# x tiles by chunk pairs, second value weights in quarters and one more warm-up matmul in the opening of a state-space and memory-attention kernel

## Chip, cores and metric

The kernel runs on one core of a Trainium2 chip. The metric is the device time of one execution in microseconds. All runs below are in the same (fast) state. The changed kernel was measured beside runs of the kernel before on the same chip.

## The reference, cut to what matters

Two independent parts, joined along the last axis. Part A is a diagonal complex state-space layer over 2048 steps. Part B is attention in segments of 32 rows with 8 memory rows, 32 heads of width 128:

```python
v = jnp.einsum('btd,dhe->bhte', h, Wv)     # h: 8 memory rows and 32 rows of x
...
o = jnp.einsum('bhqk,bhke->bhqe', p, v)
o = jnp.einsum('bhte,hed->btd', o, Wo)     # its first 8 rows are the next memory
```

The change touches only how the kernel begins, with the products of x and the value weights `Wv` for the first 512 rows of x and the first two groups of four heads.

## The kernel before

The value matmuls take x with its 1024 features on the partitions, in eight chunks of 128. For the first 512 rows the kernel loads x by rows and transposes on TensorE; later rows arrive through transposing loads. `wvs[0]` and `wvs[1]` are the value weights of the first two head groups, eight chunks of 128 KB each. Two queues issue, SyncE (`k.SP`) and ScalarE (`nc.scalar`).

```python
for t in range(4):                       # a tile of 128 rows, and two chunks of weights
    for j in range(2):
        b.load_rows(t, xr, q2[j], slice(j * 512, j * 512 + 512))
    for j in range(2):
        b.load_wv(0, wvs[0], KC, q2[j], [2 * t + j])
for j in range(2):                       # second weights, two halves of 512 KB
    b.load_wv(1, wvs[1], 2, q2[j], [j])
...                                      # parameters, memory, transposing loads of x from row 512 on
for i in range(7):                       # warm-up on constants
    k.PE.matmul(pw[:, i % 2, :], one[:, 0:128], one, start=True, stop=True)

def v_first(self, w, xr, e):             # the first four row tiles
    p = [k.ps("A") for t in range(4)]
    for t, todo in enumerate((((0, 0, 2),), ((0, 2, 4), (1, 0, 4)), ((0, 4, 6), (1, 4, 6), (2, 0, 6)),
                              ((0, 6, 8), (1, 6, 8), (2, 6, 8), (3, 0, 8)))):
        self.turn_rows(t, xr)            # 8 transposes, 2 evictions
        for tt, c0, c1 in todo:          # (tile, chunks c0 to c1)
            self.v_mm(p[tt], tt, w, range(c0, c1))
    ...
```

After `v_first` come three groups of eight matmuls on the second weights, then a 24-row matmul that turns the parameters of part A. This "parameter matmul" is the mark used below: all work in front of it belongs to the opening. That work is 56 matmuls of 512 columns (32 in `v_first`, 24 in the groups) and 32 transposes.

Of the kernel before, what the change touches and what calls it, by code (L numbers as in the profile page):

```python
# [8 lines left out]
FP32 = mybir.dt.float32  # L9
BF16 = mybir.dt.bfloat16  # L10
# [14 lines left out]
PC = 8; TB = 512; NB = 4  # L25
# [108 lines left out]
class PartA:  # L134
# [11 lines left out]
    def params(self, pool, tmp):  # L146
        k = self.k; V, S, PE, nc = k.V, k.S, k.PE, k.nc
        r24 = tmp[0:3 * PC, 1536:1664]
        pr = k.ps("O")[:, 0, :]
        PE.matmul(pr[:, 0:3 * PC], r24, k.ident[0:3 * PC, 0:3 * PC], start=True, stop=True)  # L150
        raw = pool.tile([128, 3, PC], FP32, name="a_raw", bufs=1)
        V.tensor_copy(raw[:].rearrange("p a c -> p (a c)"), pr[:, 0:3 * PC])
        lre = raw[:, 0, :]; lim = raw[:, 1, :]

        def small(name):
            return pool.tile([128, PC], FP32, name=name, bufs=1)
        dtb = pool.tile([128, PC], BF16, name="a_dtb", bufs=1)
        S.activation(dtb[:], raw[:, 2, :], ACT.Exp)
        dt = small("a_dt"); V.tensor_copy(dt[:], dtb[:])
        are = small("a_are"); V.tensor_tensor(are[:], dt[:], lre, ALU.mult)  # L160
        tht = small("a_tht"); V.tensor_tensor(tht[:], dt[:], lim, ALU.mult)
        rr = small("a_rr"); S.activation(rr[:], are[:], ACT.Exp)
        turn = small("a_turn"); V.tensor_scalar(turn[:], tht[:], 1.0 / (2.0 * math.pi), None, ALU.mult)
        fr = small("a_fr8"); V.tensor_scalar(fr[:], turn[:], MAGIC, None, ALU.add)
        V.tensor_scalar(fr[:], fr[:], MAGIC, None, ALU.subtract)
        V.tensor_tensor(fr[:], turn[:], fr[:], ALU.subtract)
        s1 = small("a_s1"); S.activation(s1[:], fr[:], ACT.Sin, scale=TWO_PI_LO)
        V.scalar_tensor_tensor(fr[:], fr[:], -1.0, fr[:], ALU.mult, ALU.max)
        c1 = small("a_c1"); S.activation(c1[:], fr[:], ACT.Sin, scale=-TWO_PI_LO, bias=k.hpb[:])
        nre = small("a_nre"); V.tensor_tensor(nre[:], rr[:], c1[:], ALU.mult)  # L170
        V.tensor_scalar(nre[:], nre[:], 1.0, None, ALU.subtract)
        nim = small("a_nim"); V.tensor_tensor(nim[:], rr[:], s1[:], ALU.mult)
        den = small("a_den"); V.tensor_tensor(den[:], lre, lre, ALU.mult)
        t0 = small("a_t0"); V.tensor_tensor(t0[:], lim, lim, ALU.mult)
        V.tensor_tensor(den[:], den[:], t0[:], ALU.add)
        V.reciprocal(den[:], den[:])
        V.tensor_scalar(den[:], den[:], 2.0, None, ALU.mult)
        bre = small("a_bre"); V.tensor_tensor(bre[:], nre[:], lre, ALU.mult)
        V.tensor_tensor(t0[:], nim[:], lim, ALU.mult)
        V.tensor_tensor(bre[:], bre[:], t0[:], ALU.add)  # L180
        V.tensor_tensor(bre[:], bre[:], den[:], ALU.mult)
        bim = small("a_bim"); V.tensor_tensor(bim[:], nim[:], lre, ALU.mult)
        V.tensor_tensor(t0[:], nre[:], lim, ALU.mult)
        V.tensor_tensor(bim[:], bim[:], t0[:], ALU.subtract)
        V.tensor_tensor(bim[:], bim[:], den[:], ALU.mult)
        nbre = small("a_nbre"); V.tensor_scalar(nbre[:], bre[:], -1.0, None, ALU.mult)
        self.rr, self.turn, self.bre, self.nbre, self.bim = rr, turn, bre, nbre, bim
        ji = pool.tile([128, TB + 1], I32, name="a_k1", bufs=1)
        k.G.iota(ji[:], pattern=[[1, TB + 1]], base=0, channel_multiplier=0)
        V.tensor_copy(self.jf, ji[:])  # L190
# [126 lines left out]
class PartB:  # L317
# [21 lines left out]
    def init(self, tmp, pm):  # L339
        k = self.k  # L340
        k.V.memset(self.accE[:], 0.0)
        m0 = tmp[0:M, 0:D]
        for c in range(KC):
            k.PE.matmul(pm[:, c * M:(c + 1) * M], tmp[0:M, c * 128:(c + 1) * 128], k.ident[0:M, 0:M], start=True, stop=True)
        self.memT = self.xe[:, :, T:XE]
        k.V.memset(self.memT, 0.0)
        k.V.tensor_copy(self.m0T[:], pm[:, 0:KC * M].rearrange("p (c m) -> p c m", c=KC))
        k.V.tensor_copy(self.memT[:, :, 0:NMX + 1], self.m0T[:])
# [19 lines left out]
            if lo < hi:  # L368
                k.SP.dma_start(self.xe[:, :, lo:hi], self.x[0][lo + r:hi + r, :], transpose=True)

    def load_rows(self, t, xr, e, cs=slice(0, D)):
        self.k.tc.keep_in_program_order(e.dma_start(xr[:, t, cs], self.x[0][t * 128 + 64:t * 128 + 192, cs]))

    def turn_rows(self, t, xr):

        k = self.k
        pt = k.ps("O", (128, 2, 1024), BF16)
        for c in range(KC):
            k.tc.keep_in_program_order(k.PE.transpose(pt[:, c // 4, (c % 4) * 128:(c % 4) * 128 + 128], xr[:, t, c * 128:(c + 1) * 128], k.ident[:]))
        for i in range(2):  # L380
            k.copy("v", self.xe[:, 4 * i:4 * i + 4, t * 128:(t + 1) * 128], pt[:, i, 0:512].rearrange("p (c n) -> p c n", c=4))

    def sum_x(self, q, pool):

# [47 lines left out]
    def v_pair(self, hb, q, w, e):  # L432
# [8 lines left out]
        self.v_st(hb, q, st, e)  # L441
        yield

    def v_first(self, w, xr, e):

        k = self.k
        p = [k.ps("A") for t in range(4)]
        for t, todo in enumerate((((0, 0, 2),), ((0, 2, 4), (1, 0, 4)), ((0, 4, 6), (1, 4, 6), (2, 0, 6)),
                                  ((0, 6, 8), (1, 6, 8), (2, 6, 8), (3, 0, 8)))):
            self.turn_rows(t, xr)  # L450
            for tt, c0, c1 in todo:
                self.v_mm(p[tt], tt, w, range(c0, c1))
        for q in range(2):
            st = self.v_tile()
            for i in range(2):
                k.copy("s", st[:, i, :], p[2 * q + i][:])
                if i == 0:
                    yield
            self.v_st(0, q, st, e)
            yield  # L460
# [409 lines left out]
def kernel_main(tc, A_x, A_Lre, A_Lim, A_Bre, A_Bim, A_Cre, A_Cim, A_logdt, A_Dskip, B_x, B_mem0, B_Wq, B_Wk, B_Wv, B_Wo, out,  # L870
                force=False, dbg=None):
    with ExitStack() as ctx:
        k = K(tc, ctx)
        k.dbg = dbg
        nc = k.nc
        consts(k)
        a = PartA(k, A_x, A_Lre, A_Lim, A_Bre, A_Bim, A_Cre, A_Cim, A_logdt, A_Dskip, out)
        b = PartB(k, B_x, B_mem0, B_Wq, B_Wk, B_Wv, B_Wo, out)
# [10 lines left out]
        with pool("p1", "right") as p1:  # L889
            tmp = a.hsp.tile([128, 2 * PC * TB], BF16, name="a_hs", bufs=4)  # L890
            w01 = a.hsp.tile([128, 2 * PC * TB], BF16, name="a_hs", bufs=4)
            wvs = {i: w01[:, 4096 * i:4096 * i + 4096].rearrange("p (a b) -> p a b", a=KC) for i in range(2)}
# [4 lines left out]
            a.jf = b.rall[:, 0:TB + 1]  # L897
            xr = tmp[:, 4096:8192].rearrange("p (t d) -> p t d", t=4)
            q2 = (k.SP, nc.scalar)
            for t in range(4):  # L900
                for j in range(2):
                    b.load_rows(t, xr, q2[j], slice(j * 512, j * 512 + 512))
                for j in range(2):
                    b.load_wv(0, wvs[0], KC, q2[j], [2 * t + j])
            for j in range(2):
                b.load_wv(1, wvs[1], 2, q2[j], [j])
            a.load_params(tmp)
            k.SP.dma_start(tmp[0:M, 0:D], b.mem0[0])
            b.load_x(512, 1024)
            b.load_x(1024, 1536)  # L910
            b.load_x(1536, T)
            one = nc.const_aps.tensor(1.0, [128, 512], BF16)
            pw = k.ps("O")
            for i in range(7):
                k.PE.matmul(pw[:, i % 2, :], one[:, 0:128], one, start=True, stop=True)

            def values():
                yield from b.v_first(wvs[0], xr, k.SP)
                for hb, q in [(1, 0), (1, 1)] + [(hb, q) for q in range(2, 8) for hb in range(2)]:
                    yield from b.v_pair(hb, q, wvs[hb], k.SP)  # L920
                for hb in range(2, HB):
                    for q in range(8):
                        if q == 1 and hb + 1 < HB and hb + 1 not in wvs:
                            wvs[hb + 1] = b.load_wv(hb + 1)
                        yield from b.v_pair(hb, q, wvs[hb], k.SP)
            v = values()
# [76 lines left out]
        with pool("p3", "right") as p3:  # L1003
            b.p3 = p3
            b.qk_init(p3)
            pr, at = b.proj(), b.attention()
# [8 lines left out]
            for n, (hp, u) in enumerate(at):  # L1015
# [4 lines left out]
                if u == 4 and 8 <= hp < 12:  # L1020
                    w = k.w8((8, 512), "wo0")
# [117 lines left out]
```

## Time and profile before

| | before |
|---|---|
| median time (first three runs) | 1241.64 us |
| span of the traced run | 1240.4 us |
| TensorE busy | 1230.1 us |
| parameter matmul starts | 20.77 us |

The profile page of the kernel before: the busy times of the engines (first line) and the shares of the chain of work that ended last (second line).

```profile
PE 1230.1 (99%) x8078; PEld 654.6 (53%) x8148; DVE 610.7 (49%) x1124; ACT 326.0 (26%) x754; POOL 211.6 (17%) x290
...
PE 98%; DMA 1%; issue 0%; DVE 0%
```

TensorE is the limit, and only 1% of the chain is a transfer. The list of TensorE waits of the kernel before, over the whole span (microseconds in total, times, longest):

```profile
PE psO L379 <- DMA a_hs<-in_B_x_dram: 0.9, 1, 0.9
PE psO L915 <- PEq L1120: 0.8, 1, 0.8
PE psS L414 <- DMA a_hs<-in_B_Wv_dram: 0.6, 1, 0.6
PE psS L414 <- DVE b_xe L77: 0.5, 1, 0.5
```

All four lie in the first 16 us. The TensorE timeline of the opening before: start, duration, operation, count, and in brackets the idle time. L915 is the warm-up, L379 a transpose, L414 a value matmul, L150 the parameter matmul.

```profile
0.85 3.07 PE L915 MATMUL psO<-const-bfloat16-1.0 128*128 128x512 bf16 x7 [0.85 <-PEq L1120]
3.76 0.62 PE L379 MATMUL psO<-ident,a_hs 128*128 128x128 bf16 x8
4.90 0.61 PE L414 MATMUL psS<-a_hs,b_xe 128*128 128x512 bf16 x2 [0.52 <-DVE b_xe L77]
6.42 0.62 PE L379 MATMUL psO<-ident,a_hs 128*128 128x128 bf16 x8 [0.92 <-DMA a_hs<-in_B_x_dram]
...
13.00 1.89 PE L414 MATMUL psP<-a_hs,b_xe 128*128 128x512 bf16 x8
15.49 1.90 PE L414 MATMUL psS<-a_hs,b_xe 128*128 128x512 bf16 x8 [0.60 <-DMA a_hs<-in_B_Wv_dram]
...
20.77 0.18 PE L150 MATMUL psO<-ident,a_hs 24*128 24x24 bf16 x1
```

Read the starts rather than the durations. At full clock a 512-wide matmul starts every 216 ns (each is recorded as 0.38 us long, so neighbours overlap), a transpose every 56 ns, as between 7.62 and 8.92 us in this trace. So after the two matmuls at 4.90 TensorE could have gone on at 5.33, and it went on at 6.42, when the second row tile had landed. One number sums up an opening:

**excess = (start of the parameter matmul - start of the first transpose) - 13.9 us**, where 13.9 = 56 x 0.216 + 32 x 0.056 is the work in between.

Before it is 20.77 - 3.76 - 13.9 = 3.1 us.

### The profile page before, as it was taken

What the parts mean: (1) busy time and instruction counts of PE and PEld (TensorE: products, weight loads), DVE (VectorE), ACT (ScalarE), POOL (GpSimd) and SP (SyncE); (2) the same over time, 40 slices, a digit from 0 to 9 for tenths busy, and PEclk for the clock granted to TensorE, in tenths of its full rate; (3) what the DMA queues carried; (4) which work ended last, traced back from release to release, by engine and by line L of the source; (5) the groups of instructions that cost most, each with busy time, mean ns of one, the idle gap of its engine ahead of it and who ended that gap; (6) DMA issues with size and microseconds to landing.
All of it is one profiled execution on the core that took longest, in us unless ns stands there. A gap on an engine that the chain in (4) does not pass through costs nothing.

```text
span 1240.4 us, 19648 instructions
## 1 busy us (share of the span) xinstructions
PE 1230.1 (99%) x8078; PEld 654.6 (53%) x8148; DVE 610.7 (49%) x1124; ACT 326.0 (26%) x754; POOL 211.6 (17%) x290
## 2 busy tenths in 40 slices
PE   8999999999999999999999999999999999999998
PEld 4444444444455445566666655655565554454444
DVE  4889999999941122444444444444444550011000
ACT  3344334444310001332333333333333230000000
POOL 2000000000032144222222222232222330000000
PEclk9999999999999999999999999999999999999999
DMA  9942232333666558577668554645575469707000
GB/s 220 261 132 66 87 94 68 102 94 77 153 187 203 154 166 164 106 151 149 134 128 170 124 136 96 128 77 104 106 139 106 73 203 218 153 18 153 17 18 28
DMA packets 306056, 153.95 MB, mean 124 GB/s; under 512 B 147242, under 2 KB 299810, under 8 KB 305962
## 3 DMA queue, kind: packets, MB, share of 16 engines
q1 hardware_dynamic: 304138, 150.82, 52.6%
q10 hardware_dynamic: 1824, 1.84, 0.5%
q8 instruction: 65, 1.06, 0.4%
q14 instruction: 29, 0.24, 0.1%
HBM read 73.70 MB, written 44.71 MB: 95 GB/s over the span
## 4 chain that ended last, share of the span: by engine, by line
PE 98%; DMA 1%; issue 0%; DVE 0%
PE psP L587 33%; PE psS L687 9%; PE psO L256 9%; PE psS L414 9%; PE psP L414 9%; PE psP L687 5%; PE psP L310 4%; PE psS L310 4%; PE psP L570 4%; PE psO L631 3%; PE psS L613 3%; PE psO L687 2%; PE psS L720 1%; PE psP L505 1%; PE psP L739 1%; DMA a_hs<-in_B_Wv_dram 1%
## 5 line engine op out<-in xcount | busy, mean ns | idle before, releaser
L587 PE MATMUL psP<-b_xe,w 128*128 128x480 bf16 x2048 | 439.3, 366 | 0.0
L587 PEld LDWEIGHTS <-w 128*128 128x128 bf16 x2048 | 193.9, 98 | 183.0
L620 POOL TENSOR_TENSOR b_m<-b_e,maskB 99x396 bf16<-99x396 bf16 x160 | 139.4, 871 | 347.5 <-ACT b_e L616 347.5
L77 DVE CAST b_q<-psP 128x480 bf16<-128x480 f32 (+1 forms) x192 | 98.0, 531 | 145.3 <-PE psP L587 133.8
L414 PEld LDWEIGHTS <-b_xe 128*128 128x128 bf16 x1024 | 99.8, 98 | 121.7 <-DMA a_hs<-in_B_Wv_dram 1.1
L75 ACT ACTIVATE b_k<-psP 128x480 bf16<-128x480 f32 x128 | 73.1, 571 | 318.7 <-PE psP L587 318.7
L687 PEld LDWEIGHTS <-b_ol 128*128 128x128 bf16 x960 | 93.1, 98 | 109.3
L616 ACT ACTIVATE b_e<-psS 99x396 bf16<-99x396 f32 x176 | 87.4, 497 | 170.5 <-PE psS L613 161.7
L638 DVE TENSOR_TENSOR b_ot<-psO,b_rall 99x512 bf16<-99x512 f32 x176 | 121.6, 691 | 6.4
L256 PE MATMUL psO<-w,a_bt 128*128 128x512 bf16 x496 | 114.7, 379 | 0.8
L636 DVE RECIPROCAL b_rall<-psO 99x4 f32<-99x4 f32 x176 | 31.1, 177 | 132.5 <-PE psO L631 132.5
L687 PE MATMUL psS<-w,b_ol 128*128 128x512 bf16 x406 | 91.5, 379 | 0.6
L414 PE MATMUL psS<-w,b_xe 128*128 128x512 bf16 x378 | 90.1, 379 | 0.4
L414 PE MATMUL psP<-w,b_xe 128*128 128x512 bf16 x376 | 89.8, 379 | 0.4
L256 PEld LDWEIGHTS <-a_bt 128*128 128x128 bf16 x512 | 49.7, 98 | 59.0
L310 PEld LDWEIGHTS <-a_hs 128*128 128x128 bf16 x512 | 49.5, 98 | 58.3
L77 DVE CAST b_ost<-psS 128x512 bf16<-128x512 f32 x13 | 9.0, 691 | 125.4 <-PE psS L687 125.4
L631 PE MATMUL psO<-b_v,b_m 128*128 128x129 bf16 x704 | 70.0, 221 | 0.0
L613 PEld LDWEIGHTS <-b_k 128*128 128x128 bf16 x704 | 50.0, 98 | 33.9 <-DVE b_k L77 0.2
L613 PE MATMUL psS<-b_q,b_k 128*128 128x99 bf16 x704 | 60.1, 208 | 0.1
L75 ACT ACTIVATE b_vst<-psS 128x512 bf16<-128x512 f32 x56 | 33.4, 597 | 99.1 <-PE psS L414 70.2
L353 POOL MEMSET b_z<- 32x128 bf16 x1 | 0.2, 194 | 341.3 <-DVE a_hs L292 341.3
(205 smaller groups left out, 1162.3 us busy)
## 6 DMA issues: line engine op xcount, KB each, us to landing
b_v<-b_vx SPq DMA_DIRECT2D x16, 1056.0 KB
b_os<-b_ot SPq DMA_DIRECT2D x16, 960.0 KB
w<-in_B_Wv_dram SPq DMA_DIRECT2D x14, 1024.0 KB
b_vx<-b_vst SPq DMA_DIRECT2D x48, 256.0 KB
w<-in_B_Wo_dram SPq DMA_DIRECT2D x12, 1024.0 KB
w<-in_B_Wq_dram SPq DMA_DIRECT2D x16, 512.0 KB
w<-in_B_Wk_dram SPq DMA_DIRECT2D x16, 512.0 KB
a_xn<-in_A_x_dram SPq DMA_DIRECT2D x32, 128.0 KB
```

The costliest lines, as they stand in the source:

```text
L75: self.S.activation(out, in_, ACT.Copy)
L77: self.V.tensor_copy(out, in_)
L256: m = PE.matmul(u[:, i, :], self.bt[:, i, c, :], self.xT[tb][:, c, :], start=(c == 0), stop=(c == KC - 1))
L310: PE.matmul(py[:], self.hs[tb][:, pc, i, tt * 128:(tt + 1) * 128], self.ct[half, i][:, pc, :], start=(pc == 0 and i == 0), stop=(pc == PC ...
L414: m = self.k.PE.matmul(p[:], self.xe[:, c, t * 128:(t + 1) * 128], w[:, c, :], start=(c == 0), stop=(c == KC - 1))
L587: PE.matmul(p[:, 0:480], w[:, i * KC + c, hh * 128:(hh + 1) * 128], self.xe[:, c, 480 * q:480 * q + 480], start=(c == 0), stop=(c == KC - 1))
L613: PE.matmul(s[:, j * GW:(j + 1) * GW], kt[:, hh, g0:g0 + 128], qt[:, hh, g0:g0 + GW], start=True, stop=True)
L616: k.S.activation(e[:], s[0:GW, 0:4 * GW], ACT.Exp, scale=float(E) ** -0.5, accum_out=self.accE[0:GW, i:i + 1])
L620: k.G.tensor_tensor(v4(m[0:GW, 0:4 * GW]), v4(e[:]), mask[0:GW, :, :].unsqueeze(2).to_broadcast([GW, 2, 2, GW]), ALU.mult)
L631: PE.matmul(o[:, gg, cs], m[:, j * GW:j * GW + 128], vt[:, 2 * u + gg, cs], start=True, stop=True)
L638: V.tensor_tensor(ot[:, 2 * u:2 * u + 2, :].rearrange("p g (h e) -> p g h e", h=2), oa[:, :, 1:257].rearrange("p g (h e) -> p g h e", h=2) ...
L687: k.PE.matmul(self.acc[t, half], ol[:, h8, tt * 128:(tt + 1) * 128], self.wo_half(half, h), start=(h == 0), stop=(h == H - 1))
```

## The change

The intent is to have every 512 KB that lands bring as much work as it can. x arrives by pairs of chunks for 256 rows at a time, beside the two chunks of weights that go with it; the later pairs come in wider pieces. The second weights come in four pieces in the order in which they are used. A warm-up matmul stands in the wait for the first eviction, so that TensorE stays busy until then (4.29 to 4.68 us in the trace below).

```diff
-    def load_rows(self, t, xr, e, cs=slice(0, D)):
-        ... xr[:, t, cs] <- self.x[0][t * 128 + 64:t * 128 + 192, cs]
+    def load_rows(self, j, q, xr, e, n=1):
+        cs = slice(256 * q, 256 * (q + n))
+        ... xr[:, 2 * j:2 * j + 2, cs] <- self.x[0][256 * j + 64:256 * j + 320, cs].rearrange("(i p) d -> p i d", p=128)
...
+    def warm(self, n): ...               # one matmul of n columns on constants
     def v_first(self, w, xr, e):
-        for t, todo in enumerate(...): ...
+        for c in range(2):
+            self.turn_rows(0, 0, xr, c, 1)
+        self.warm(384)
+        for q in range(4):
+            if q > 0:
+                self.turn_rows(1, q, xr)
+            for t in range(2):
+                self.v_mm(p[t], t, w, (2 * q,))
+            if q == 0:
+                self.turn_rows(1, q, xr)
+            for t in range(2):
+                self.v_mm(p[t], t, w, (2 * q + 1,))
+            if q < 3:
+                self.turn_rows(0, q + 1, xr)
+            for t in range(2, 4):
+                self.v_mm(p[t], t, w, range(2 * q, 2 * q + 2))
...
-            for t in range(4):
-                (two halves of row tile t, then weight chunks 2t and 2t + 1)
-            for j in range(2):
-                b.load_wv(1, wvs[1], 2, q2[j], [j])
+            for q in range(4):
+                for j in range(2):
+                    if q < 3:
+                        b.load_rows(j, q, xr, q2[j], 1 + q // 2)
+                    b.load_wv(0, wvs[0], KC, q2[1 - j], [2 * q + j])
+            for j in range(4):
+                b.load_wv(1, wvs[1], 4, q2[j % 2], [j])
```

The diff is cut: lines in brackets and after "..." stand for longer code. The rest of it pins some small matmuls to program order and moves the warm-up to another PSUM tile.

More of the change, by code (lines that the diff above doesn't have):

```diff
@@ L149, in params @@
         pr = k.ps("O")[:, 0, :]
-        PE.matmul(pr[:, 0:3 * PC], r24, k.ident[0:3 * PC, 0:3 * PC], start=True, stop=True)
+        k.tc.keep_in_program_order(PE.matmul(pr[:, 0:3 * PC], r24, k.ident[0:3 * PC, 0:3 * PC], start=True, stop=True))
         raw = pool.tile([128, 3, PC], FP32, name="a_raw", bufs=1)
@@ L343, in init @@
         for c in range(KC):
-            k.PE.matmul(pm[:, c * M:(c + 1) * M], tmp[0:M, c * 128:(c + 1) * 128], k.ident[0:M, 0:M], start=True, stop=True)
+            k.tc.keep_in_program_order(
+                k.PE.matmul(pm[:, c * M:(c + 1) * M], tmp[0:M, c * 128:(c + 1) * 128], k.ident[0:M, 0:M], start=True, stop=True))
         self.memT = self.xe[:, :, T:XE]
@@ L369, in load_x, with turn_rows @@
                 k.SP.dma_start(self.xe[:, :, lo:hi], self.x[0][lo + r:hi + r, :], transpose=True)
-    def load_rows(self, t, xr, e, cs=slice(0, D)):
-        self.k.tc.keep_in_program_order(e.dma_start(xr[:, t, cs], self.x[0][t * 128 + 64:t * 128 + 192, cs]))
-    def turn_rows(self, t, xr):
-        k = self.k
-        pt = k.ps("O", (128, 2, 1024), BF16)
-        for c in range(KC):
-            k.tc.keep_in_program_order(k.PE.transpose(pt[:, c // 4, (c % 4) * 128:(c % 4) * 128 + 128], xr[:, t, c * 128:(c + 1) * 128], k.ident[:]))
-        for i in range(2):
-            k.copy("v", self.xe[:, 4 * i:4 * i + 4, t * 128:(t + 1) * 128], pt[:, i, 0:512].rearrange("p (c n) -> p c n", c=4))
+    def load_rows(self, j, q, xr, e, n=1):
+        cs = slice(256 * q, 256 * (q + n))
+        self.k.tc.keep_in_program_order(e.dma_start(
+            xr[:, 2 * j:2 * j + 2, cs], self.x[0][256 * j + 64:256 * j + 320, cs].rearrange("(i p) d -> p i d", p=128)))
+    def turn_rows(self, j, q, xr, c0=0, n=2):
+        k = self.k
+        pt = k.ps("O", (128, 2, 256), BF16)
+        for c in range(n):
+            for i in range(2):
+                cs = 256 * q + 128 * (c0 + c)
+                k.tc.keep_in_program_order(k.PE.transpose(
+                    pt[:, c, i * 128:i * 128 + 128], xr[:, 2 * j + i, cs:cs + 128], k.ident[:]))
+        k.copy("v", self.xe[:, 2 * q + c0:2 * q + c0 + n, 256 * j:256 * j + 256], pt[:, 0:n, :])
     def sum_x(self, q, pool):
@@ L442, in v_pair, with warm @@
         yield
+    def warm(self, n):
+        k = self.k
+        one = k.nc.const_aps.tensor(1.0, [128, n], BF16)
+        k.tc.keep_in_program_order(k.PE.matmul(self.pw[:, 0, 0:n], one[:, 0:128], one, start=True, stop=True))
     def v_first(self, w, xr, e):
@@ L447, in v_first @@
         p = [k.ps("A") for t in range(4)]
-        for t, todo in enumerate((((0, 0, 2),), ((0, 2, 4), (1, 0, 4)), ((0, 4, 6), (1, 4, 6), (2, 0, 6)),
-                                  ((0, 6, 8), (1, 6, 8), (2, 6, 8), (3, 0, 8)))):
-            self.turn_rows(t, xr)
-            for tt, c0, c1 in todo:
-                self.v_mm(p[tt], tt, w, range(c0, c1))
+        for c in range(2):
[14 more added lines that the diff above has]
+                self.v_mm(p[t], t, w, range(2 * q, 2 * q + 2))
         for q in range(2):
@@ L899, in kernel_main @@
             q2 = (k.SP, nc.scalar)
-            for t in range(4):
+            for q in range(4):
                 for j in range(2):
-                    b.load_rows(t, xr, q2[j], slice(j * 512, j * 512 + 512))
-                for j in range(2):
-                    b.load_wv(0, wvs[0], KC, q2[j], [2 * t + j])
-            for j in range(2):
-                b.load_wv(1, wvs[1], 2, q2[j], [j])
+                    if q < 3:
[3 more added lines that the diff above has]
+                b.load_wv(1, wvs[1], 4, q2[j % 2], [j])
             a.load_params(tmp)
@@ L911, in kernel_main @@
             b.load_x(1536, T)
-            one = nc.const_aps.tensor(1.0, [128, 512], BF16)
-            pw = k.ps("O")
-            for i in range(7):
-                k.PE.matmul(pw[:, i % 2, :], one[:, 0:128], one, start=True, stop=True)
+            b.pw = k.psp.tile([128, 1, 512], FP32, name="psS", bufs=2)
+            for n in 7 * (512,):
+                b.warm(n)
             def values():
```

## The prediction

> **What bounds the kernel now.** TensorE. It is busy 1230.1 of 1240.4 us (first table of the profile), and the chain of waits is 98% TensorE. The only TensorE waits of any size lie before 16 us. So only the opening can be shortened, and what is saved there should pass straight through to the end.
>
> **The opening, from the TensorE timeline.** Seven warm-up matmuls run from 0.85 us, 427 ns apart. The first x tile lands at 3.71 and its transposes start at 3.76. The 24-row parameter matmul, behind three further groups of eight, stands at 20.77. Between the two, the starts show these holes beyond the normal spacing (216 ns for a 512-wide matmul, 56 for a transpose): 0.68 us at 4.90 (eviction of the transposes), 1.08 at 6.42 (second x tile), 0.31 at 7.18 (eviction), 0.76 at 15.49 (second value weights, whose two 512 KB pieces land around 15.4). Sum about 2.8 us. The rest is work.
>
> The cause is arrival order. x and the first weights (2 MB) are in by 11.7 us, the third MB by 15.4. With row tiles little can be computed from the first 512 KB: one tile and two chunks.
>
> **What the change does.** Bytes are the same. Each chunk pair now brings 256 KB of x and 256 KB of weights, good for eight matmuls and eight transposes: 8 x 0.216 + 8 x 0.056 = 2.2 us of TensorE against about 2.2 us of transfer. So TensorE stays about level with the transfers.
> Added: one 384-wide warm matmul (0.16 us, inside a wait), nine evictions in place of eight (0.42 us each, on an idle VectorE), 512-byte packets for half of x. Packets of 1 KB took 46 ns and of 256 B 18 ns in this trace; for 512 B I estimate 27 ns, about 0.07 us more per 128 KB piece. [...] There are still 18 loads, about eight in flight.
>
> **Left after it**, if arrivals by cumulative bytes stay: about 0.55 us for the first eviction, 0.5-0.8 for the second chunk pair of x (around 6.2), 0-0.5 for the wide pieces of x (around 10), nothing for the second weights (first quarter in by 12.5, needed at 14). That leaves 1.1-1.8 of the 2.8 us. One new limit: the transposing load of x rows from 512 on lands at 20.6 and is first used at 22.82; more than 2.2 us of gain would run into it.
>
> TensorE's clock is up by 3.8 us. [...]
>
> **Prediction.** A gain of about 1.5 us, 0.12%: 1240.1 us, 8 in 10 between 1239.0 and 1241.3. Faster by over 2%: 0.01; within 2%: 0.98; slower by over 2%: 0.01.
>
> **What would show it.** The 24-row parameter matmul at about 19.2 instead of 20.77; first value matmuls at about 4.5; no wait for the second value weights; x chunk waits under 1 us in sum; the rest of the trace the same, shifted.
>
> **What would make it wrong.** Narrow packets slower than assumed, or the wide x pieces landing late, so that chunk waits eat the gain; a wait for the transposing load of x at 20.6; a later stage tied to absolute DMA times; warm-up matmuls delaying the first transposes.

Two sentences that did not rest on this case's traces are cut where marked; neither was a term of the sum, which is 2.8 us of holes less the 1.1 to 1.8 left, that is 1.0 to 1.7, put as about 1.5. For the clock the trace of the kernel before shows the first record of full granted clock at 3.71 us, and full clock from there to 1239.34 us, over holes of up to 1.08 us. The figures of what is left are estimates from the landing times of that trace, the 2.2 us of transfer is 512 KB at its 238 GB/s (mean of the first 60 us), and the 27 ns lies between its 18 and 46 in proportion to the bytes. The eight loads in flight are shown under the experiments.

## The result, and the profile after

| | before | after |
|---|---|---|
| median (six runs each) | 1241.76 us | 1240.84 us |
| range | 1241.46 to 1242.03 | 1240.21 to 1241.27 |
| mean | 1241.77 | 1240.82 |
| span of the traced run | 1240.4 | 1238.5 |

The ratio is 0.9992, with an interval of 0.9979 to 1.0005. The gain of the means is 0.95 us here, and 0.91 and 1.23 us in two later sets (e1 and e9 below). By medians it is 0.92, 0.74 and 0.99 us (the kernel before has single slow runs, up to 1243.06 in the set of e9). All of this is smaller than the stated interval of one set; that the effect is real rests on its coming back in three sets, and on the traces. In two of the three sets every run of the changed kernel is faster than every run of the kernel before; in that of e1 they overlap by 0.07 us.

The page of the changed kernel, busy times and chain as above:

```profile
PE 1230.3 (99%) x8079; PEld 654.6 (53%) x8149; DVE 611.3 (49%) x1125; ACT 325.5 (26%) x754; POOL 211.6 (17%) x290
...
PE 99%; issue 0%; DVE 0%
```

The transfers have left the chain. The waits of TensorE and of its weight loads (which run ahead of it: those for the transposes at 5.12 us start at 4.90) in the changed kernel, over the whole span:

```profile
PE psS L454 <- PEq L1142: 0.8, 1, 0.8
...
PEld L385 <- DMA a_hs<-in_B_x_dram: 2.1, 4, 0.8
...
PEld L420 <- DVE b_xe L77: 0.3, 1, 0.3
```

The 2.1 us belong to weight loads that wait while matmuls still run; little of it reaches TensorE (the holes of 0.2 and 0.14 us below). The TensorE timeline of the opening after (L454 warm-up, L385 transpose, L420 value matmul):

```profile
0.85 3.15 PE L454 MATMUL psS<-const-bfloat16-1.0 128*128 128x512 bf16 x7 [0.85 <-PEq L1142]
3.90 0.61 PE L385 MATMUL psO<-ident,a_hs 128*128 128x128 bf16 x4
4.29 0.50 PE L454 MATMUL psS<-const-bfloat16-1.0 128*128 128x384 bf16 x1
4.68 0.39 PE L420 MATMUL psS<-a_hs,b_xe 128*128 128x512 bf16 x1
...
7.77 0.38 PE L420 MATMUL psP<-a_hs,b_xe 128*128 128x512 bf16 x1
8.19 0.40 PE L385 MATMUL psO<-ident,a_hs 128*128 128x128 bf16 x4
...
13.13 0.59 PE L420 MATMUL psP<-a_hs,b_xe 128*128 128x512 bf16 x2
13.56 1.89 PE L420 MATMUL psS<-a_hs,b_xe 128*128 128x512 bf16 x8
...
18.84 0.18 PE L150 MATMUL psO<-ident,a_hs 24*128 24x24 bf16 x1
```

The first value matmul starts at 4.68, and from there holes are small: 0.2 us at 8.19 (7.77 + 0.22 is 7.99), 0.14 at 9.43. The group at 13.56 starts 0.43 us after the pair at 13.13, with no wait for the second weights. The excess is 18.84 - 3.90 - 13.9 = 1.0 us, against 3.1.

So the traces differ by 1.93 us at the parameter matmul and by 1.9 us in span. But the mean times differ by 0.95 us only. The traced run of the changed kernel was the fastest of its six (1240.21), and the traced run of the kernel before (1242.15) was slower than all six timed runs listed for it. The experiments ask what the gain consists of and why the traces show twice as much of it.

### The profile page after: what moved, and what is told of

Same layout as the page of the kernel before. It is cut to its first block, busy times and chain, and to the rows that moved or that the text cites. A ratio compares the mean times of both kernels' runs of the same rounds, so it can differ in the third digit from the quotient of the medians.

```text
span 1238.5 us, 19651 instructions
## 1 busy us (share of the span) xinstructions
PE 1230.3 (99%) x8079; PEld 654.6 (53%) x8149; DVE 611.3 (49%) x1125; ACT 325.5 (26%) x754; POOL 211.6 (17%) x290
## 3 DMA queue, kind: packets, MB, share of 16 engines
q8 instruction: 65, 1.06, 0.4%
## 4 chain that ended last, share of the span: by engine, by line
PE 99%; issue 0%; DVE 0%
PE psP L610 33%; PE psS L710 9%; PE psS L420 9%; PE psO L256 9%; PE psP L420 9%; PE psP L710 5%; PE psP L310 4%; PE psS L310 4%; PE psP L593 4%; PE psO L654 3%; PE psS L636 3%; PE psO L710 2%; PE psS L743 1%; PE psP L528 1%; PE psP L762 1%; PE psO L505 1%
## 5 line engine op out<-in xcount | busy, mean ns | idle before, releaser
L420 PEld LDWEIGHTS <-b_xe 128*128 128x128 bf16 x1024 | 99.7, 98 | 119.1 <-DVE b_xe L77 0.3
L420 PE MATMUL psS<-w,b_xe 128*128 128x512 bf16 x378 | 90.1, 379 | 0.4
L420 PE MATMUL psP<-w,b_xe 128*128 128x512 bf16 x376 | 89.8, 379 | 0.4
```

Of the source, the lines that this page charges most:

```text
L420: m = self.k.PE.matmul(p[:], self.xe[:, c, t * 128:(t + 1) * 128], w[:, c, :], start=(c == 0), stop=(c == KC - 1))
```

## The experiments

All kernels passed the comparison with the reference. "Clock rise" is the start of the trace's first record of full granted TensorE clock; it is also seen in the timeline as the spacing of 512-wide matmuls going from 427 to 216 ns. (PEclk on the page and in `--windows` doesn't show it: it reads full before the rise too, as before 3.71 us in the kernel before.) Landing times come from the trace's record of transfer completions, 16 for each piece; the last of them counts.

Two things in these records are used by the expectations. Pieces land unevenly: in the kernel before, 13 of the 16 completions of the two halves of the second row tile were in by 5.29 and 5.52 us, and the last three came at 6.09 to 6.15 and 6.31 to 6.37. (That each of the 16 belongs to one transfer engine is my reading; the records don't name it.) And eight loads are in flight: in the changed kernel the first eight are issued from 0.81 to 2.30 us without waiting for a landing, and each of the ten after them 0.01 to 0.03 us after the last completion of an earlier one (the ninth at 3.48, after 3.45).

Two theories. **D (arrivals)**: what is left in the opening, and its spread, comes from pieces of x and weights that land late. **C (clock)**: TensorE now works from 3.9 us on, so the moment of the clock rise, which differs from run to run of one kernel, costs time that the earlier waits used to hide. The half microsecond for each microsecond that the expectations give it is an estimate from the spacings of 427 and 216 ns; e12 against e9, below, gives 0.36.

The table has every traced run (us). "Total" is the time of that very run; "mean" is of all runs of the set (in the first row, of the six runs beside "after"; its traced run is from an earlier set of three), and the last column is that mean minus the mean of the kernel before in the same set.

| kernel | first transpose | clock rise | parameter matmul | excess | total | mean | against before |
|---|---|---|---|---|---|---|---|
| before | 3.76 | 3.71 | 20.77 | 3.1 | 1242.15 | 1241.77 | |
| e8 before again | 3.79 | 5.85 | 21.11 | 3.4 | 1242.49 | 1241.79 | +0.08 |
| after | 3.90 | 4.64 | 18.84 | 1.0 | 1240.21 | 1240.82 | -0.95 |
| e1 after again | 4.05 | 5.64 | 19.01 | 1.1 | 1240.38 | 1240.71 | -0.91 |
| e9 after, third | 4.05 | 4.44 | 18.77 | 0.8 | 1240.16 | 1240.48 | -1.23 |
| e2 quarters only | 3.79 | 5.33 | 20.86 | 3.2 | 1242.76 | 1241.89 | +0.27 |
| e3 no quarters | 3.95 | 5.05 | 19.30 | 1.5 | 1240.74 | 1241.05 | -0.57 |
| e4 all narrow | 4.06 | 5.93 | 19.15 | 1.2 | 1240.96 | 1241.73 | +0.11 |
| e10 narrow again | 4.04 | 3.46 | 18.68 | 0.7 | 1240.56 | 1241.39 | -0.31 |
| e5 floor | 4.02 | 6.51 | 19.38 | 1.5 | 1240.74 | 1240.44 | -1.27 |
| e7 no 384 warm-up | 4.05 | 3.65 | 19.79 | 1.8 | 1241.16 | 1240.94 | -0.77 |
| e11 wide weights | 4.00 | 6.54 | 20.53 | 2.6 | 1241.97 | 1241.68 | -0.03 |
| e12 one warm-up | 4.10 | 7.27 | 19.79 | 1.8 | 1241.59 | 1241.65 | -0.06 |

(e6, with 24 warm-up matmuls, is told below.) In all fourteen traces the time from the start of the parameter matmul to the start of the last matmul is 1215.80 or 1215.81 us. So nothing after the opening reacts to the change in any trace: the total is the opening, plus a constant, plus the program's end.

**The program's end.** From the start of the last matmul to the landing of the last store it took 2.03 to 2.05 us in twelve traces, 2.46 in e12 and 3.16 in e6. From there to the end of the span it took 1.80 to 1.88 us in eleven traces and 2.24 to 2.25 in e4, e10 and e2. These three are the kernels with 20 early loads in place of 18. Their traces show why. SyncE closes the program by waiting on its transfer semaphores one after another, about 0.07 us each. With 18 loads the last store's semaphore is the last of that row: one wait is left after it lands. With 20 it is the seventh from the end, and the row ends 0.44 us later (waits at +0.02 to +0.46). With 16 loads (e3 and e11) three are left. So comparing kernels with another number of transfers carries up to 0.4 us that have nothing to do with the opening. Before and after have the same number.

**e1, the changed kernel again**

> The changed kernel once more, for its mean, its spread and a second trace. In the first trace the granted clock rose at 4.64 us (before: 3.71), after the first four transposes, and that run was the fastest of six (1240.21; the others up to 1241.27). Theory C (clock): the opening now has TensorE at work from 3.9 us without long waits, so each microsecond that the clock rises later costs about half a microsecond of the total, and this makes the wider spread; the 24-row parameter matmul stands later than 18.84 us by half of (clock rise - 4.64). Theory D (arrivals): the spread comes from chunk pieces that land late on single transfer engines; the parameter matmul then stands later by the sum of the waits for x and weights in the trace, whenever the clock rose. Mean 1240.8 either way.

Measured: median 1240.78 (1240.38 to 1241.08). The clock rose a microsecond later than in the first trace, and the parameter matmul came only 0.17 us later: 0.15 of that was a later start, and two matmuls and some transposes at the low clock cost 0.4 us, which then vanished because the waits at 8.19 and 9.43 were not needed any more. So a late rise is partly hidden behind arrivals; neither theory alone fits. The second trace was again the fastest of its set.

**e2, the kernel before with quarters only**

```diff
-            for j in range(2):
-                b.load_wv(1, wvs[1], 2, q2[j], [j])
+            for j in range(4):
+                b.load_wv(1, wvs[1], 4, q2[j % 2], [j])
```

> The kernel before with only the second value weights in four pieces in order of need. The hole of 0.76 us at 15.49 should vanish and nothing else: 1241.0, parameter matmul at 20.0. If the gain of the change lies in the x tiles alone, 1241.7.

Measured: median 1241.69. Its timeline where the second weights had been missing:

```profile
11.66 0.38 PE L414 MATMUL psS<-a_hs,b_xe 128*128 128x512 bf16 x1
12.78 0.38 PE L414 MATMUL psS<-a_hs,b_xe 128*128 128x512 bf16 x1 [0.74 <-DMA a_hs<-in_B_Wv_dram]
```

The wait at 15.49 is gone, as expected (the group after it starts with no wait, at 15.58), but one of 0.9 us (12.78 - 11.66 - 0.22) stands at 12.78, for the last chunk of the first weights, which landed at 12.74 here and at 11.66 in the kernel before. The wait has moved rather than gone, and the parameter matmul came at 20.86 where I expected 20.0. Of the time, 0.43 us is the longer end described above; without it the mean (1241.89) would lie 0.2 us under that of before, so at most a small part of the gain. My expectation of 1241.0 failed; the other one, 1241.7, was met.

**e3, the changed kernel with halves**

```diff
-            for j in range(4):
-                b.load_wv(1, wvs[1], 4, q2[j % 2], [j])
+            for j in range(2):
+                b.load_wv(1, wvs[1], 2, q2[j], [j])
```

> The changed kernel with the second value weights in two halves of 512 KB as before. With quarters the last piece landed at 13.15 us, before its first use at 13.56, so if halves land as early nothing is lost: 1240.8. If halves land at 15.4 as in the kernel before, a wait of up to 1.8 us comes back: 1242.

Measured: median 1240.97. Its timeline at the first group on the second weights:

```profile
12.96 0.59 PE L420 MATMUL psP<-a_hs,b_xe 128*128 128x512 bf16 x2
14.02 1.90 PE L420 MATMUL psS<-a_hs,b_xe 128*128 128x512 bf16 x8 [0.46 <-DMA a_hs<-in_B_Wv_dram]
```

The halves landed at 13.55 and 13.97, and TensorE was ready at 13.39: a wait of 0.63 us, between my two cases. The mean is 0.34 us above e1. So the chunk pairs make most of the gain (0.57 us remain without quarters). The quarters do nothing much by themselves; once the chunk pairs let TensorE arrive earlier they save a wait that this trace shows. That this is a third of a microsecond in the mean is not shown: five runs each, with ranges of 1.0 and 0.7 us, barely resolve it.

**e4 and e10, all pieces of x narrow**

```diff
-                    if q < 3:
-                        b.load_rows(j, q, xr, q2[j], 1 + q // 2)
+                    b.load_rows(j, q, xr, q2[j])
```

> The changed kernel with the last two chunk pairs of x as narrow 128 KB pieces too (20 loads in place of 18). My estimate of 0.07 us for a narrow piece, and the waits of 0.2 and 0.3 us for the wide pieces at 8.19 and 9.43: within 0.3 us of the changed kernel. If width matters for the issue limit (eight in flight), the second weights come later and it loses 0.5 us or more.

> The kernel with all pieces of x narrow once more: its mean was 1241.73, 1.0 us above the changed kernel, while its trace showed no wait for x after 4.1 us and the parameter matmul at 19.15. If width matters: again 0.7 us or more above e9, and a trace with waits for chunk pieces of 0.5 us or more. If that was chance of the runs: within 0.4 of e9.

Measured: medians 1241.63 (e4) and 1241.09 (e10), that is 0.85 and 0.63 us above the changed kernel in the same set. By means it is 1.02 and 0.91 us. The openings of both traces are about as good as the changed kernel's (19.15 and 18.68). 0.43 us of the difference is the longer end, seen in both traces: half or more of it by medians, under half by means. The rest is in no trace; e10 also has one run of 1243.41. So neither of my cases came true as stated: the kernel loses more than 0.5 us, but its traces have no wait for late pieces that would be the reason (0.2 us at most, in e10). What the width of the pieces is worth stays open; what is shown is the part that belongs to the number of transfers.

**e5, a floor without waits for loads** (wrong values on purpose)

```diff
-                    pt[:, c, i * 128:i * 128 + 128], xr[:, 2 * j + i, cs:cs + 128], k.ident[:]))
+                    pt[:, c, i * 128:i * 128 + 128], xr[:, i, 128 * (c0 + c):128 * (c0 + c) + 128], k.ident[:]))
...
-    self.v_mm(p[t], t, w, (2 * q,))            # and the other v_mm of v_first
+    self.v_mm(p[t], t, w, (2 * q,), 0)         # always chunk 0 of the first weights
-    for hb, q in [(1, 0), (1, 1)] + [...]:
+    for hb, q in ((1, 0), (1, 1)):             # the same for the first groups after it
+        yield from b.v_pair(hb, q, wvs[0], k.SP, 0)
...
-    V.tensor_copy(self.flag[:], ok[:, 3:4])
+    V.memset(self.flag[:], 0)                  # stay off the slow path
```

> Wrong result on purpose: the changed kernel with the same loads, but the transposes of the opening read only the first piece of x and the first 16 + 24 - 8 = 48 + further matmuls of the first five groups' worth of work read only the first chunk of the first value weights (v_first and the two first pairs of the second head group), so that after the first pieces TensorE waits for no load until the rows from 512 on. The flag for the slow path is held at zero. From the first trace: 4.68 + 32 x 0.216 + 28 x 0.056 + 24 x 0.216 = 18.3 for the parameter matmul, against 18.84 and 19.01, so 0.5 us is all that arrivals still cost in the traced runs. In all timed runs so far of the changed kernel the first, traced, one was the fastest and the later ones 0.1 to 1.1 us slower. Theory D (arrivals): here all runs come out at 1239.8 within 0.3. Theory C (clock): the later runs stay as far above the first as they do for the changed kernel, 0.3 to 0.6 on average.

(The clause "16 + 24 - 8 = 48 + further" in that text is a slip. What is meant is that all matmuls of `v_first` and of the four groups of the two pairs after it read the first chunk of the first weights.) The values are wrong, yet the comparison passed, so it doesn't watch this part closely.

Measured: 1240.74, 1240.03, 1240.66, 1240.00, 1240.78. Its opening, where no load is waited for after the first pieces:

```profile
4.80 0.61 PE L420 MATMUL psS<-a_hs,b_xe 128*128 128x512 bf16 x1
5.20 0.63 PE L420 MATMUL psP<-a_hs,b_xe 128*128 128x512 bf16 x1
5.62 0.63 PE L385 MATMUL psO<-ident,a_hs 128*128 128x128 bf16 x4
6.05 0.61 PE L420 MATMUL psS<-a_hs,b_xe 128*128 128x512 bf16 x1
6.48 0.40 PE L420 MATMUL psP<-a_hs,b_xe 128*128 128x512 bf16 x1
...
19.38 0.18 PE L150 MATMUL psO<-ident,a_hs 24*128 24x24 bf16 x1
```

The starts at 4.80, 5.20, 5.62, 6.05 and 6.48 stand 0.40 to 0.43 us apart (those at 4.80, 5.20 and 6.05 are 512-wide matmuls that take 0.22 at full clock), and only from about 6.5 on, where the clock rises, is the spacing of matmuls 0.22. The parameter matmul comes at 19.38, later than in all three traces of the changed kernel although nothing waits for loads. That is theory C at work, in a run with a late rise. Theory D's claim that all runs would agree within 0.3 us fails (0.78 us between them). Theory C's claim fails as stated too: the later runs were not slower than the first, because the first had the late rise itself. On average the floor is 1.27 us under the kernel before and the changed kernel 0.91 to 1.23 (0.91 on the same chip), so by these means late arrivals cost the changed kernel about 0 to 0.4 us, a difference within their noise.

**e6, 24 warm-up matmuls in place of 7**

```diff
-            for n in 7 * (512,):
+            for n in 24 * (512,):
```

> The changed kernel with 24 initial warm-up matmuls in place of 7, so that TensorE reaches the transposes at about 0.5 x (clock rise) + 5.6 us = 7.9 to 8.6, when most loads are in. The parameter matmul should stand near 8.2 + 14.4 = 22.6 and the total near 1244, which also tests that a shift of the opening passes through whole. Theory C: the spread over the runs stays, since each microsecond of clock rise still costs half a microsecond. Theory D: the spread shrinks to that of the program's end, about 0.4.

(The 7.9 to 8.6 is an estimate: 24 matmuls from 0.85 us on, 427 ns apart before a clock rise at 4.64 to 5.93 us, as in the earlier traces of the changed kernel and its variants, and 216 ns after it.)

Measured: 1245.29 (traced), 1244.63, 1245.52, 1244.45, 1244.50; parameter matmul at 22.73, clock rise at 5.35. The 3.9 us that the opening is longer than in the first trace of the changed kernel arrive whole at the last matmul (1238.54 against 1234.65). So a shift of the opening does pass through. The question of the spread stays undecided here: 1.1 us of the traced run is a last store that landed 3.16 us after the last matmul in place of 2.04.

**e7, without the 384-wide warm-up**

```diff
             self.turn_rows(0, 0, xr, c, 1)
-        self.warm(384)
```

> The changed kernel without the one 384-wide warm-up matmul between the first transposes and the first value matmuls. It fills an eviction wait and takes no time of its own, so if the clock doesn't depend on it: 1240.8, same. [...]

Measured: median 1241.01 (1240.51 to 1241.21), mean 0.77 us under the kernel before, as against 0.91 for e1 on the same chip: no difference that these runs resolve. In its trace the clock had risen at 3.65, before the place of this matmul, so the trace says nothing about its use. (The other case of my expectation, a later clock rise and a loss, is cut where marked: it rested on a mechanism that no run here shows.) It does show what a late piece costs:

```profile
8.68 0.59 PE L420 MATMUL psP<-a_hs,b_xe 128*128 128x512 bf16 x2
10.38 0.40 PE L385 MATMUL psO<-ident,a_hs 128*128 128x128 bf16 x4 [1.10 <-DMA a_hs<-in_B_x_dram]
```

Here a wide piece of x is waited for until 10.38, 1.3 us, in a place where the changed kernel's three traces have waits of 0 to 0.14 us. This is theory D in the same opening.

**e8, the kernel before again**

> The kernel before once more, for a second trace and its spread. Its first, traced, run was 1242.15, slower than the untraced ones (1241.46 to 1242.03), the reverse of the changed kernel. If the traced run is always the slow one here (about 0.5 us above the mean of the others), the two first traces overstate the gain: 1.9 us between them against 0.9 us between the means. If it is chance, the traced run falls anywhere within 1241.0 to 1242.2.

Measured: 1242.49 (traced), 1242.08, 1241.85, 1240.81, 1241.71. Again the traced run is the slowest. Its clock rose at 5.85, two microseconds later than in the first trace. The first transposes took 1.06 us here and 0.62 in the first trace, and the first value matmuls came 0.47 us later (5.37 against 4.90). In its timeline:

```profile
3.79 1.06 PE L379 MATMUL psO<-ident,a_hs 128*128 128x128 bf16 x8
5.37 0.82 PE L414 MATMUL psS<-a_hs,b_xe 128*128 128x512 bf16 x2 [0.52 <-DVE b_xe L77]
...
15.82 1.90 PE L414 MATMUL psS<-a_hs,b_xe 128*128 128x512 bf16 x8 [0.67 <-ACT a_hs L75]
...
21.11 0.18 PE L150 MATMUL psO<-ident,a_hs 24*128 24x24 bf16 x1
```

None of the delay reaches the parameter matmul by itself: both traces then wait for the second weights, which landed at 15.44 and 15.77 (the view names ScalarE here, but the landing is 0.05 us before the start), and the parameter matmuls are the same 0.33 us apart. The opening of the kernel before follows its last arrival and hides the clock.

**e9, the changed kernel a third time**

> The changed kernel a third time, as the anchor of this set and for a third trace. In all ten traces so far the time from the parameter matmul to the last matmul was 1215.81 us, so the total is its start plus 1215.8 + 2.0 + 1.8 + 1.7 with some tenths of the program's end: 1221.4 plus its start. Two traces of the kernel before have it at 20.77 and 21.11, two of the changed kernel at 18.84 and 19.01, but the mean times differ by 0.95 us only, so the means want it near 20.3 and 19.5. If the traces so far were lucky ones: this trace has it between 18.8 and 20.0, with the clock rise anywhere between 3.6 and 6.6 us, and mean 1240.8.

Measured: median 1240.46 (1240.16 to 1240.91), traced run fastest once more, parameter matmul at 18.77, just under the range that I gave.

**e11, four weight chunks in two wider loads**

```diff
-                    b.load_wv(0, wvs[0], KC, q2[1 - j], [2 * q + j])
+                    if q < 2:
+                        b.load_wv(0, wvs[0], KC, q2[1 - j], [2 * q + j])
+                    elif j == 0:
+                        b.load_wv(0, wvs[0], 4, q2[3 - q], [q])
```

> The changed kernel with the last four chunks of the first value weights in two loads of two chunks (16 loads in place of 18). If fewer and wider later loads are what helps (eight in flight, the issuing queue waiting for earlier landings): 0.2 to 0.5 us below e9, which would be the fastest version. If only the bytes count: same as e9 within 0.3; if the coarser pieces make TensorE wait: up to 0.4 above.

Measured: median 1241.77, mean 1.2 us above e9: no better version, and outside all three of my cases. In its trace the clock rose late (6.54) and a wide piece of x landed at 11.07, after 9.32 to 9.43 for its place in the changed kernel:

```profile
9.55 0.59 PE L420 MATMUL psP<-a_hs,b_xe 128*128 128x512 bf16 x2
11.12 0.40 PE L385 MATMUL psO<-ident,a_hs 128*128 128x128 bf16 x4 [0.97 <-DMA a_hs<-in_B_x_dram]
```

Fewer and wider loads are not what helps by itself; with coarser pieces beside it, x came later. That the wider weights delayed it is likely but not shown: e7 had such a late piece with the unchanged loads.

**e12, one warm-up matmul in place of seven**

```diff
-            for n in 7 * (512,):
+            for n in (512,):
```

> The changed kernel with one initial warm-up matmul in place of seven: TensorE idles from 1.3 us until the first piece lands. Theory C: the clock rises one busy stretch after the transposes start, at 6.7 to 9.6 us instead of 3.6 to 6.6 as seen so far, and at half a microsecond per microsecond this costs 1.0 to 1.5 us, the waits for pieces of x hiding a little: 1241.8 to 1242.3 and a parameter matmul at 20 to 20.6. If arrivals set the opening: same as e9 within 0.4.

(The 6.7 to 9.6 is an estimate: the 2.8 to 5.7 us from the first matmul to the clock rise that the traces had shown until then, counted here from a first transpose at 3.9.)

Measured: median 1241.59 (1241.43 to 1242.19), mean 1.17 us above e9, parameter matmul at 19.79; the clock rose at 7.27. The direction and the range of the rise are as theory C has them, the size is a little under its range (1241.8 to 1242.3; 20 to 20.6). The first value matmuls and the transposes between them, first e12:

```profile
4.88 0.61 PE L420 MATMUL psS<-a_hs,b_xe 128*128 128x512 bf16 x1
5.28 0.63 PE L420 MATMUL psP<-a_hs,b_xe 128*128 128x512 bf16 x1
5.71 0.63 PE L385 MATMUL psO<-ident,a_hs 128*128 128x128 bf16 x4
6.14 0.63 PE L420 MATMUL psS<-a_hs,b_xe 128*128 128x512 bf16 x1
```

and e9:

```profile
4.84 0.39 PE L420 MATMUL psS<-a_hs,b_xe 128*128 128x512 bf16 x1
5.07 0.38 PE L420 MATMUL psP<-a_hs,b_xe 128*128 128x512 bf16 x1
5.28 0.39 PE L385 MATMUL psO<-ident,a_hs 128*128 128x128 bf16 x4
5.50 0.38 PE L420 MATMUL psS<-a_hs,b_xe 128*128 128x512 bf16 x1
```

Both start their first transpose within 0.05 us of each other (4.10 and 4.05); by the third value matmul e12 is 0.64 us behind, at the parameter matmul 1.0 us. A rise 2.8 us later cost 1.0 us, 0.36 us for each. The seven warm-up matmuls, which look like idle work, are worth about as much as the whole change.

## Why the prediction was right or wrong

The time was inside the range (1240.84 in 1239.0 to 1241.3), and "within 2%" was right. That says little by itself: the range is 2.3 us wide, and a gain of half a microsecond would have been inside it too. The mechanism, a shorter opening that passes straight through, was right. The gain was 0.9 to 1.2 us by means where 1.5 was said. That 1.5 lies between the means and the 1.9 us of the traces is in part luck, as far as the sums below go: two errors, told below, pull in opposite ways.

- *"What is saved there should pass straight through to the end"*: right in every trace, to 0.01 us. All fourteen have 1215.8 us from the parameter matmul to the last matmul, while the parameter matmul itself moved between 18.68 and 22.73.
- *Holes of 2.8 us before, 1.1 to 1.8 left after*: in the traces more was saved than said. The excess went from 3.1 and 3.4 us to 1.0, 1.1 and 0.8; the parameter matmul came at 18.8 to 19.0 where 19.2 was said. The wait for the second chunk pair, put at 0.5 to 0.8, doesn't show in the first trace: its two pieces of x landed at 5.50 and 6.82 us and were turned from 5.77 and 6.90 on, without a wait. The waits for x there are 0.2 and 0.14 us, under the 1 us in sum that was said.
- *Narrow packets*: 27 ns was the estimate and 27 ns the median measured for 512-byte packets, against 46 for 1 KB. (The trace of the kernel before has such packets too, over 100,000 of them from 410 us on, with the same median; its opening has none.) By these two numbers a narrow piece took 17% more transfer time than the same bytes in 1 KB packets (2 x 27 against 46). The medians in the two first traces, 18 ns for 256 B, 27 for 512 B, 46 for 1 KB and 84 for 2 KB, lie within 1 ns of 9 ns plus 37 ns for each KB.
- *No wait for the second weights*: right in all three traces. The last of the four pieces landed at 13.15, 14.52 and 13.01, each before its use.
- *First value matmuls at about 4.5*: 4.68 to 4.84.
- *The limit at 2.2 us from the transposing load*: nothing of it was measurable; even with the parameter matmul at 18.68 (e10) the rest kept its 1215.81.

The term that seems mis-sized is the 2.8 us itself: the prediction took the holes of one trace for the holes of the kernel. The support for this is a sum, not a trace. A run of the kernel before of 1240.83 us, as one set has, leaves at most 1240.83 - 1215.81 - 2.04 - 1.80 - 1.71 = 19.5 us in front of the parameter matmul (with the shortest end and surplus over the span seen in the traces), where the traces have 20.8 and 21.1. If the constants hold in that run, its second weights came more than a microsecond earlier than in the traces, and then there is less to save. The same sum on the means of the three sets gives 20.3 to 20.4 us for the kernel before, 0.4 to 0.9 less than its traces, and 19.1 to 19.5 for the changed kernel, 0.3 to 0.6 more than the trace of the same set: an estimate by which both kernels have a share in the difference. The prediction also left out a term: it said that the clock is up by 3.8 us, as in the one trace (there 2.86 us after the first matmul), but it rose between 3.46 and 6.54 us in the twelve traces with seven warm-up matmuls, that is 2.6 to 5.7 us after the first matmul (three traces of the one changed kernel have 4.64, 5.64 and 4.44), and a later rise costs the changed kernel time (0.36 us for each microsecond in e12 against e9) where the kernel before waits anyhow.

What stays open is why the traced runs show the gain at its largest. The difference of the traced runs is about 2.1 us (1242.15 and 1242.49 against 1240.21, 1240.38 and 1240.16), that of the means 0.9 to 1.2. In all five sets of the changed opening in its plain form or with narrow pieces (after, e1, e9, e4, e10) the traced run was the fastest, and for the row-tile opening (before, e2, e8) the slowest. The traced run is also the first of its set (in every set whose list has it), so being first and being traced can't be told apart. The pattern is too regular for chance to be a comfortable answer, and the other variants (e3, e5, e6, e7, e11, e12) don't follow it. The untraced runs show only their time, so their arrivals and their clock can't be read.

## What to carry to other kernels

When an engine is busy 99% of the time, as here, and its work stays the same, look at the opening and the end. A mark in the program (here the parameter matmul) with the constant time behind it separates them from everything else. Order first loads so that each piece that lands brings equal work to the engine that is the limit; order alone moves waits around when the bytes in front of them haven't come (in e2 a wait of 0.76 us at 15.49 became one of 0.9 us at 12.78). For effects of a microsecond one trace is one draw: take the mean of many runs, and check whether the number of transfers has moved the program's end (by 0.43 us here).
